# A convolution in four blocks beside an FFN: a loaded spectrum used twice, and a spectrum kept in the tile of the normalised x

## The chip, the cores and the metric

The kernel runs on one core of a Trainium2 chip. The metric is the device time of one execution in microseconds (us). Before the change it is 1384.04 us, the median of 3 runs (1380.11 to 1387.81). Several engines work side by side on the core, each with its own queue of instructions in a fixed order: TensorE (PE) multiplies matrices into PSUM, VectorE (DVE) and ScalarE (ACT) do elementwise work, GpSimd (POOL) and SyncE (SP) here mostly issue transfers between memory and the on-chip buffers.

## The reference

One input x of 2048 tokens with 576 features goes through two residual parts, each behind a layernorm with a scale and a shift (`ca`, `sa`, `ga` and so on come from a small product of `c` with `w_mod`):

```
h = layernorm(x) * (1 + ca) + sa
x = x + ga * (irfft(rfft(h, 4096) * rfft(K, 4096))[:2048] + h * D_skip)
h = layernorm(x) * (1 + cb) + sb
x = x + gb * (relu(h @ w1) @ w2)
```

The convolution runs along the tokens, one kernel K (2048 long) for each feature, built from the parameters `log_A_real`, `A_imag`, `C_real`, `C_imag` and `log_dt`. `w1` is 576 x 4608, `w2` is 4608 x 576. All is float32.

## The kernel before

The tokens are cut into four blocks of 512 (NB = 4). The convolution of block s needs block s and all earlier ones: it is a sum over t = 0 to s of products of a spectrum of K with a spectrum of block t of the normalised x. `conv(s)` (lines 847 to 953) does this in two halves of the features, p = 0 and 1:

- `norm1` writes the normalised x into `h` (a tile with the tag "h", one buffer, 2304 floats for each partition, in a pool `hb` of its own).
- `transform` multiplies it on PE with a matrix of cosines and sines (`ps_f`), ACT copies the result to `Z`, and `butterfly` on DVE makes `W` and then the spectrum `U_s_p`; the same for the piece of K, then `K_s_p`. Every operation of DVE in these helpers has line 509.
- `spec_K` also loads `R`, the spectrum of the piece of K before (from `Rd[s-1][p]`), and makes `K2` out of R and K (lines 887 and 889).
- `product(p, Y)` sums over pairs (Ka, Ua) in the order t = 0, s, 1, ..., s-1. For each pair it makes `T = Ka*Ua` and `Y = Y +- T` on DVE; the first pair writes two of its four products straight to Y. What is not at hand is loaded: `Ka` from `Kd` (`Kd[0]` is the same memory as `Rd[0]`) and `Ua` from `Ud`.
- `back` makes `V` from Y, `inverse` multiplies it on PE (`ps_i`, line 983, one PSUM buffer), and DVE adds each of the four results to x. Then `norm2` prepares the block for the FFN.

All spectra, Z, W, Y and V, and the loaded R, Ka and Ua, are tiles with the tag "S" (1152 KB) in a pool with 6 buffers (line 728). A tile takes the next buffer of the six and waits until its former owner has been read for the last time, by a store too. `load` (line 736) and `save` (line 740) are transfers issued by POOL.

The FFN of a block runs through 36 steps. Step g does `first(g)`: 14 matmuls into a PSUM tile `hps` (line 1284, two buffers), ACT makes `hh`, the relu rounded (line 1289), DVE makes the rest `hl` from hps and hh (line 1290), which frees the hps. Two steps later `second` does 14 matmuls of hh and hl with w2 into five accumulators (line 1309). During the first block DVE also splits each weight into a high and a low part (`w<-r,w`, line 509: one operation of 640 columns for w1; two, of 64 and 512, for w2), and SP stores the low parts for the later blocks (`L1d`, `L2d`, line 1364).

`conv(1)` runs beside the FFN of block 0, `conv(2)` beside that of block 1, `conv(3)` beside that of block 2; `conv(s)` is a generator out of which the FFN draws a few operations at each half step. The scheduler of the language then sets the order of each engine's queue, by priorities and by the times that it reckons with, so that a change of what an operation waits for can change the order too.

Of the kernel before, what the change touches and what calls it, by code (L numbers as in the profile page):

```python
# [10 lines left out]
F32 = mybir.dt.float32  # L11
# [7 lines left out]
P = 128  # L19
# [4 lines left out]
NB = 4  # L24
# [5 lines left out]
PC = 288  # L30
# [456 lines left out]
class Body:  # L487
# [359 lines left out]
    def conv(self, s):  # L847

        nc = self.nc
        v = nc.vector.tensor_tensor  # L850
        xp = self.xp[s % 2]
        x2 = self.x2p[s % 2].tile([P, 4, D], F32, tag="x2", bufs=1, name=f"x2_{s}")
        self.x2[s] = x2
        nc.gpsimd.dma_start(out=x2, in_=self.I["x"][s].rearrange("n m d -> m n d"))
        kt = [self.load_kt(s, 0), None]
        yield -1
        yield -1
        if s > 1:
            self.h = self.hb.tile([P, 4, D], F32, tag="h", name=f"h_{s}")
        h = self.h  # L860
        hv = h.rearrange("m n (dd p q) -> m n dd p q", dd=4, p=2)

        def mm_U(p, Z):
            return self.transform(lambda n2: hv[:, n2, :, p], self.fcU, Z)

        def mm_K(p, Z):
            ktv = kt[p].rearrange("p (t dd g) q -> p t dd g q", t=2, g=2)
            return self.transform(lambda n2: ktv[:, n2 // 2, :, n2 % 2], self.fcK, Z)

        def spec_U(p, Z):  # L870
            U = self.spec(f"U_{s}_{p}")
            yield from self.butterfly(Z, U, -1)
            yield -1
            if s + 1 < NB or p == 1:
                self.save(self.Ud[s][p], U)
            Us.append(U if p == 0 else None)

        def spec_K(p, Z):
            R = self.load(self.Rd[s - 1][p], "R")
            K = self.spec(f"K_{s}_{p}")  # L880
            yield from self.butterfly(Z, K, -1)
            yield -1
            if s + 1 < NB:
                self.save(self.Rd[s][p], K)
            f = nc.vector.scalar_tensor_tensor
            K2 = self.spec(f"K2_{s}_{p}")
            f(K2[:, :, 0], R[:, :, 1], self.sgn[:, 1:2], K[:, :, 0], op0=ALU.mult, op1=ALU.add)
            yield 1.35
            f(K2[:, :, 1], R[:, :, 0], self.sgn[:, 0:1], K[:, :, 1], op0=ALU.mult, op1=ALU.add)
            yield 1.35  # L890
            yield -1
            if s + 1 < NB:
                self.save(self.Kd[s][p], K2)
            Ks.append(K2)

        def product(p, Y):
            def pair(t):
                Ka = Ks[p] if t == 0 else self.load(self.Kd[s - t][p], "Ka")
                Ua = Us[p] if (t == s and Us[p] is not None) else self.load(self.Ud[t][p], "Ua")
                return Ka, Ua  # L900

            order = [0, s, *range(1, s)]
            nxt = pair(0)
            yield -1
            for i, t in enumerate(order):
                Ka, Ua = nxt
                if i + 1 < len(order):
                    nxt = pair(order[i + 1])
                yield from self.product(Y, Ka, Ua, i == 0)

        def inverse(p, V):
            ops = lambda n2: [(self.gc[:, n2, c, :], V[:, n2, c]) for c in range(2)]
            return self.inverse(x2, p, ops)

        def back(p, Y):
            V = self.spec(f"V_{s}_{p}")
            yield from self.butterfly(Y, V, 1)
            Vs.append(V)

        Us, Ks, Vs = [], [], []  # L920
        if s == 1:
            ZU = self.spec("Z")
            yield from mm_U(0, ZU)
            Z1 = self.spec("Z")
            yield from both(spec_U(0, ZU), mm_U(1, Z1))
            ZK = self.spec("Z")
            yield from both(spec_U(1, Z1), mm_K(0, ZK))
            kt[1] = self.load_kt(s, 1)
            yield from spec_K(0, ZK)
            ZK = self.spec("Z")  # L930
            Y = self.spec(f"Y_{s}_0")
            yield from both(product(0, Y), mm_K(1, ZK))
        else:
            ZK = self.spec("Z")
            yield from both(self.norm1(x2, h), mm_K(0, ZK))
            kt[1] = self.load_kt(s, 1)
            ZU = self.spec("Z")
            yield from both(spec_K(0, ZK), mm_U(0, ZU))
            Z1 = self.spec("Z")
            yield from both(spec_U(0, ZU), mm_U(1, Z1))  # L940
            ZK = self.spec("Z")
            yield from both(spec_U(1, Z1), mm_K(1, ZK))
            Y = self.spec(f"Y_{s}_0")
            yield from product(0, Y)
        yield from back(0, Y)
        yield from both(spec_K(1, ZK), after(3, inverse(0, Vs[0])))
        Y = self.spec(f"Y_{s}_1")
        yield from product(1, Y)
        yield from back(1, Y)
        yield -1  # L950
        yield -1
        yield from inverse(1, Vs[1])
        yield from self.norm2(s, x2, xp)
# [510 lines left out]
def after(n, g):  # L1464

    for _ in range(n):
        yield 0.0
    yield from g


def both(a, b):

    while True:
        n = 0
        for g in (a, b):
            for w in g:
                n = 1
                yield w
                break
        if not n:  # L1480
            return
# [58 lines left out]
```

## Time and profile before

| | us |
|---|---|
| median of 3 runs | 1384.04 (1380.11 to 1387.81) |
| the profiled execution | 1382.06 |
| its span in the profile | 1380.3 |
| PE busy | 1233.1 |
| DVE busy | 869.9 |
| ACT busy | 503.1 |
| POOL busy | 197.9 |

The profile is one execution, recorded by the hardware. Rows of a timeline give the start and the length in us, the engine, the line, the operation with what it writes and reads, and in brackets how long the engine was idle before and what ended that. "x2" means two such instructions in a row. Rows of waits give the sum, the number of times and the longest. The row of a window gives busy times and counts of PE, PE's weight loads, DVE, ACT and POOL, then the granted clock of PE as a share of full speed, the busy share of the DMA engines and GB/s. The mean clock over the span is 0.939. Where the FFN of block 0 runs with `conv(1)` beside it, up to about 565 us, DVE is the busier engine; from about 640 us on PE is busy nearly all the time.

### The profile page before, as it was taken

The page shows a single profiled execution, that of the slowest core. Times are in us where ns is not written, and L with a number is a line of the kernel's source. Part 1 is how long each engine was busy: PE and PEld are TensorE (multiplying, and loading weights), DVE is VectorE, ACT ScalarE, POOL GpSimd, SP SyncE. Part 2 cuts the span into 40 slices and gives each one's busy share as a digit, 9 for nine tenths or more (in the row PEclk, how much of TensorE's full clock was granted, in tenths as well). Part 3 has the DMA queues.
Part 4 walks back from the last instruction along what each step waited for, and adds up shares of the span by engine and source line. Part 5 has one row for each costly group of instructions (what it writes and reads, how often), then busy time and mean ns, then how long its engine had stood idle before and what let it go on. Part 6 is the DMA issues. An engine that isn't in the chain of part 4 may idle for free.

```text
span 1380.3 us, 26042 instructions
## 1 busy us (share of the span) xinstructions
PE 1233.1 (89%) x10608; PEld 977.5 (71%) x10608; DVE 869.9 (63%) x1351; ACT 503.1 (36%) x1014; POOL 197.9 (14%) x275
## 2 busy tenths in 40 slices
PE   5124778999999987989999999999999999999998
PEld 3123556777777766667777877777877878888886
DVE  5976977999886698559834987264999232111111
ACT  7985233222224322522234324433322253222231
POOL 1776222111121100021010010000010000000000
PEclk9555787999999999899999999999999999999999
DMA  6666399788888949598788995676998657666651
GB/s 193 240 242 239 101 331 364 271 314 306 283 317 282 334 157 337 164 353 316 238 279 304 323 369 179 204 240 210 365 323 299 202 152 212 198 198 193 205 172 60
DMA packets 134568, 347.55 MB, mean 252 GB/s; under 512 B 22448, under 2 KB 22768, under 8 KB 134448
## 3 DMA queue, kind: packets, MB, share of 16 engines
q1 hardware_dynamic: 106256, 218.36, 48.6%
q0 software_dynamic: 27904, 126.94, 25.2%
q8 instruction: 83, 1.36, 0.4%
q10 hardware_dynamic: 288, 0.59, 0.1%
q14 instruction: 37, 0.30, 0.1%
HBM read 264.44 MB, written 81.40 MB: 251 GB/s over the span
## 4 chain that ended last, share of the span: by engine, by line
PE 67%; DVE 18%; DMA 7%; issue 5%; ACT 3%; POOL 1%; SPq 0%; DVEq 0%; ACTq 0%; POOLq 0%
PE acc L1309 25%; PE hps L1284 25%; PE kps L440 5%; DVE Y L509 4%; PE ps_f L749 4%; DVE T L509 4%; PE kps L262 3%; DMA Ua<-Ud 2%; PE ps_i L983 2%; DVE W L509 2%; DMA Ud<-U 1%; DVE k L133 1%; DVE hl L1290 1%; PE kps L606 1%; DMA wm_gb<-in_w_mod_dram 1%
## 5 line engine op out<-in xcount | busy, mean ns | idle before, releaser
L1309 PE MATMUL acc<-hh,w 128*128 128x512 f32 x1296 | 424.2, 401 | 6.2 <-DVE w L509 6.1
L1284 PE MATMUL hps<-xh,w 128*128 128x512 f32 x1152 | 392.0, 400 | 0.6 <-issue 0.4
L1309 PEld LDWEIGHTS acc<-hh,w 128*128 128x128 f32 x1296 | 243.0, 189 | 60.3 <-DVE w L509 7.8
L1309 PE MATMUL acc<-hl,w 128*128 128x512 f32 x720 | 278.9, 399 | 0.0
L1290 DVE SCALAR_TENSOR_TENSOR hl<-hps,hh 128x512 fp32r<-128x512 f32 x144 | 98.7, 686 | 281.5 <-ACT hh L1289 281.4
L1284 PEld LDWEIGHTS hps<-xh,w 128*128 128x128 f32 x1152 | 214.8, 188 | 47.1 <-ACT xh L1046 1.1
L1284 PE MATMUL hps<-xl,w 128*128 128x512 f32 x576 | 229.0, 397 | 0.2 <-DVE xl L1051 0.2
L1289 ACT ACTIVATE hh<-hps 128x512 fp32r<-128x512 f32 x144 | 86.0, 597 | 336.4 <-PE hps L1284 335.9
L1262 ACT ACTIVATE w<-r 128x576 fp32r<-128x576 f32 x144 | 98.7, 686 | 219.1 <-issue 172.5
L1309 PEld LDWEIGHTS acc<-hl,w 128*128 128x128 f32 x720 | 135.3, 188 | 28.3
L1284 PEld LDWEIGHTS hps<-xl,w 128*128 128x128 f32 x576 | 108.2, 188 | 24.4 <-DVE xl L1051 1.2
L1255 ACT ACTIVATE w<-r 128x640 fp32r<-128x640 f32 x142 | 104.0, 732 | 18.7 <-DMA r<-in_w_dram 18.6
L262 PE MATMUL kps<-W,W 128*32 128x16 f32 x2304 | 40.0, 218 | 78.1 <-POOL W L59 49.7
L1284 PE MATMUL hps<-xs,w 128*128 128x512 f32 x288 | 95.5, 412 | 5.4 <-DVE hl L1290 5.4
L262 PEld LDWEIGHTS kps<-W,W 128*32 128x32 f32 x2304 | 37.6, 151 | 82.7 <-POOL W L59 51.0
L440 PEld LDWEIGHTS kps<-W1r,W2r 128*32 128x32 f32 x3456 | 69.0, 146 | 31.7 <-issue 17.6
L509 DVE TENSOR_TENSOR Y<-Y,T 128x1152 f32<-128x1152 f32 x64 | 84.9, 1349 | 0.2
L440 PE MATMUL kps<-W1r,W2r 128*32 128x48 f32 (+2 forms) x3456 | 78.3, 238 | 7.3 <-DVE W1r L412 4.2
L750 ACT ACTIVATE Z<-ps_f 128x288 f32<-128x288 f32 x104 | 42.4, 408 | 64.3 <-PE ps_f L749 63.7
L1284 PEld LDWEIGHTS hps<-xs,w 128*128 128x128 f32 x288 | 52.6, 188 | 18.3 <-DVE hl L1290 7.1
L509 DVE TENSOR_TENSOR w<-r,w 128x512 fp32r<-128x512 f32 (+2 forms) x108 | 57.9, 571 | 8.7 <-ACT w L1262 8.7
L509 DVE TENSOR_TENSOR W<-Z 128x576 f32<-128x576 f32 x52 | 37.0, 751 | 28.9 <-ACT Z L750 28.9
(214 smaller groups left out, 1381.7 us busy)
## 6 DMA issues: line engine op xcount, KB each, us to landing
r<-in_w_dram SPq DMA_DIRECT2D x144, 320.0 KB, 4.4
r<-in_w_dram SPq DMA_DIRECT2D x144, 288.0 KB, 3.8
w<-L1d SPq DMA_DIRECT2D x108, 320.0 KB, 3.0
w<-L2d SPq DMA_DIRECT2D x108, 288.0 KB, 3.2
W2r<-W2d POOLq DMA_DIRECT2D x18, 1536.0 KB, 9.3
W2d<-W SPq DMA_DIRECT2D x12, 1536.0 KB, 7.8
Ua<-Ud POOLq DMA_DIRECT2D x15, 1152.0 KB, 11.1
W<-W1d POOLq DMA_DIRECT2D x18, 768.0 KB, 8.9
```

The lines of the kernel that those rows point to most:

```text
L262: self.nc.tensor.matmul(ps[32 * dd : 32 * dd + 32, 12 * u + q, :], W2[:, r, :, ch], W1[:, u, :, r, ch], start=(r == 0), stop=(r == 1),)
L440: nc.tensor.matmul(ps[32 * dd : 32 * dd + 32, q, :], W2[:, r, :, ch], W1[:, :na, r, ch], start=(r == 0), stop=(r == 1),)
L509: return self.kept(self.nc.vector.tensor_tensor(*args, **kw))
L749: kept(nc.tensor.matmul(o, fc[:, n2, c, :], src(n2), start=True, stop=True))
L750: nc.scalar.activation(Z[:, n2, c], ps[:, :PC], AF.Copy)
L983: self.nc.tensor.matmul(ps[:, :PC], a, b, start=(i == 0), stop=(i == len(todo) - 1))
L1255: nc.scalar.activation(w[:, 0], r, AF.Copy)
L1262: nc.scalar.activation(w[:, 0:D], r2[g], AF.Copy)
L1284: nc.tensor.matmul(ps, a, x, start=(i == 0), stop=(i == 13))
L1289: nc.scalar.activation(hh, ps, AF.Relu)
L1290: nc.vector.scalar_tensor_tensor(hl, ps, 0.0, hh, op0=ALU.max, op1=ALU.subtract)
L1309: nc.tensor.matmul(acc[i], a, x, start=(f == 0 and j in (0, 3, 6, 9, 12)), stop=(f == NF - 1 and j in (2, 5, 8, 11, 13)),)
```

## The change

Three things change, all in `conv(s)`. First, in block 1 (s = 1) the second pair's Ka is the same memory as the R that `spec_K` has loaded; R is now kept and used, and nothing is loaded. Second, for each s the U of the second half (p = 1) is made in a tile of the tag "h", where the normalised x lay until the transforms had read it, and stays there for `product(1)`, which loaded it again from `Ud` before. It takes no buffer of the pool of six any more. Third, U_3_1 is no longer stored, as nobody loads it.

```
         def spec_U(p, Z):
-            U = self.spec(f"U_{s}_{p}")
+            if p:
+                U = self.hb.tile([P, 4, 2, PC], F32, tag="h", name=f"U_{s}_{p}")
+            else:
+                U = self.spec(f"U_{s}_{p}")
             yield from self.butterfly(Z, U, -1)
             yield -1
-            if s + 1 < NB or p == 1:
+            if s + 1 < NB:
                 self.save(self.Ud[s][p], U)
-            Us.append(U if p == 0 else None)
+            Us.append(U)
 
         def spec_K(p, Z):
             R = self.load(self.Rd[s - 1][p], "R")
+            Rs.append(R)
...
             def pair(t):
-                Ka = Ks[p] if t == 0 else self.load(self.Kd[s - t][p], "Ka")
-                Ua = Us[p] if (t == s and Us[p] is not None) else self.load(self.Ud[t][p], "Ua")
+                if t == 0 or s == 1:
+                    Ka = (Rs if t else Ks)[p]
+                else:
+                    Ka = self.load(self.Kd[s - t][p], "Ka")
+                Ua = Us[p] if t == s else self.load(self.Ud[t][p], "Ua")
                 return Ka, Ua
...
-        Us, Ks, Vs = [], [], []
+        Us, Ks, Rs, Vs = [], [], [], []
```

The order of the queues moves with it, in three places. Lines after the change are 4 to 7 higher than before (hl is line 1297, hps 1291, acc 1316, ps_i 990).

DVE, second half of block 1, from the x add of the first half's last `ps_i` on; before, `Ua_5956` is the first pair's U, `hl_6049` and `hl_6108` belong to steps 31 and 32 of the FFN:

```order
L509 TENSOR_TENSOR x2_1_5272<-ps_i_5944,x2_1_5272 128x4x72
L509 TENSOR_TENSOR T_5996<-K2_1_1_5913,Ua_5956 128x1152
L509 TENSOR_TENSOR T_6006<-K2_1_1_5913,Ua_5956 128x1152
L509 TENSOR_TENSOR w1_5995<-r1_5958,w1_5995 128x640
L1290 SCALAR_TENSOR_TENSOR hl_6049<-hps_6030,hh_6048 128x512
L509 TENSOR_TENSOR w2_6080<-r2_5960,w2_6080 128x64
L509 TENSOR_TENSOR w2_6080<-r2_5960,w2_6080 128x512
L509 TENSOR_TENSOR w1_6052<-r1_6018,w1_6052 128x640
L509 TENSOR_TENSOR Y_1_1_5955<-K2_1_1_5913,Ua_5956 128x4x288 x2
L509 TENSOR_TENSOR Y_1_1_5955<-Y_1_1_5955,T_5996 128x4x288
L509 TENSOR_TENSOR Y_1_1_5955<-Y_1_1_5955,T_6006 128x4x288
L1290 SCALAR_TENSOR_TENSOR hl_6108<-hps_6086,hh_6107 128x512
```

The same place after; `hl_6043` belongs to step 31, and R and U_1_1 are read where Ka and a second Ua were loaded:

```order
L509 TENSOR_TENSOR x2_1_5272<-ps_i_5942,x2_1_5272 128x4x72
L509 TENSOR_TENSOR Y_1_1_5953<-K2_1_1_5911,Ua_5954 128x4x288 x2
L509 TENSOR_TENSOR T_5990<-K2_1_1_5911,Ua_5954 128x1152
L509 TENSOR_TENSOR T_6000<-K2_1_1_5911,Ua_5954 128x1152
L509 TENSOR_TENSOR Y_1_1_5953<-Y_1_1_5953,T_5990 128x4x288
L509 TENSOR_TENSOR Y_1_1_5953<-Y_1_1_5953,T_6000 128x4x288
L509 TENSOR_TENSOR T_6010<-R_5846,U_1_1_5471 128x1152
L509 TENSOR_TENSOR w1_5989<-r1_5956,w1_5989 128x640
L509 TENSOR_TENSOR Y_1_1_5953<-Y_1_1_5953,T_6010 128x4x288
L509 TENSOR_TENSOR T_6033<-R_5846,U_1_1_5471 128x1152
L1297 SCALAR_TENSOR_TENSOR hl_6043<-hps_6024,hh_6042 128x512
```

The hl of step 31 stood behind two products and one w; now it stands behind nine products and one w. The hl of step 32 follows five more products, three w and four W later.

PE at the same place, before (`hps_6144` is the first half of step 33; it takes the PSUM buffer of step 31, which hl_6049 frees):

```order
L1309 MATMUL acc4_0_3041<-hl_5992,w2_5964 128x512
L1284 MATMUL hps_6144<-xs_0_2781,w1_5995 128x512 x2
L1284 MATMUL hps_6144<-xh_0_2779,w1_5995 128x512
L1284 MATMUL hps_6144<-xl_0_2780,w1_5995 128x512
L1284 MATMUL hps_6144<-xh_0_2779,w1_5995 128x512 x2
L1284 MATMUL hps_6144<-xl_0_2780,w1_5995 128x512
L1284 MATMUL hps_6144<-xh_0_2779,w1_5995 128x512 x2
L1284 MATMUL hps_6144<-xl_0_2780,w1_5995 128x512
L1284 MATMUL hps_6144<-xh_0_2779,w1_5995 128x512 x2
L1284 MATMUL hps_6144<-xl_0_2780,w1_5995 128x512
L1284 MATMUL hps_6144<-xh_0_2779,w1_5995 128x512
L1309 MATMUL acc0_0_3037<-hh_6048,w2_6024 128x512 x2
```

And after (`hps_6138` is step 33, which takes the PSUM buffer that hl_6043 frees):

```order
L1316 MATMUL acc4_0_3041<-hl_5986,w2_5962 128x512
L1316 MATMUL acc0_0_3037<-hh_6042,w2_6018 128x512 x2
L1316 MATMUL acc1_0_3038<-hh_6042,w2_6018 128x512 x2
L1316 MATMUL acc2_0_3039<-hh_6042,w2_6018 128x512 x2
L1316 MATMUL acc3_0_3040<-hh_6042,w2_6018 128x512 x2
L1316 MATMUL acc4_0_3041<-hh_6042,w2_6018 128x512
L1291 MATMUL hps_6138<-xs_0_2781,w1_5989 128x512 x2
```

Nine matmuls with the hh of step 31 now come ahead of the hps of step 33, and those with its hl behind it.

DVE in block 2, at the end of `spec_K(1)` where the first half's result is added to x; before:

```order
L887 SCALAR_TENSOR_TENSOR K2_2_1_8558<-R_8489,sgn_203,K_2_1_8491 128x4x288
L1290 SCALAR_TENSOR_TENSOR hl_8541<-hps_8521,hh_8540 128x512
L509 TENSOR_TENSOR x2_2_7715<-ps_i_8546,x2_2_7715 128x4x72
L889 SCALAR_TENSOR_TENSOR K2_2_1_8558<-R_8489,sgn_203,K_2_1_8491 128x4x288
L509 TENSOR_TENSOR x2_2_7715<-ps_i_8560,x2_2_7715 128x4x72
```

And after:

```order
L891 SCALAR_TENSOR_TENSOR K2_2_1_8552<-R_8483,sgn_203,K_2_1_8485 128x4x288
L893 SCALAR_TENSOR_TENSOR K2_2_1_8552<-R_8483,sgn_203,K_2_1_8485 128x4x288
L1297 SCALAR_TENSOR_TENSOR hl_8535<-hps_8515,hh_8534 128x512
L509 TENSOR_TENSOR x2_2_7709<-ps_i_8540,x2_2_7709 128x4x72
L509 TENSOR_TENSOR x2_2_7709<-ps_i_8554,x2_2_7709 128x4x72
```

The first x add now stands behind both K2 operations instead of one. On POOL, the Ka of block 2's second pair is now issued ahead of the store of U_2_1, which came first before. In block 3 the last two x adds of the first half stand one product later, and the last `ps_i` three matmuls later.

## The prediction

> **What bounds the kernel now.** I read the page's first part first, then the waits of PE in stretches, then the timelines around the waits. First the busy times of the whole span:
>
> ```profile
> PE 1233.1 (89%) x10608; PEld 977.5 (71%) x10608; DVE 869.9 (63%) x1351; ACT 503.1 (36%) x1014; POOL 197.9 (14%) x275
> ```
>
> PE is busy for 89% of 1380.3 us, so a time can only be won where PE is idle or slow. The change touches the convolutions of blocks 1 to 3, which run beside the FFN of blocks 0 to 2. These are all the waits of PE that matter there (line, what it waited for, us, times, longest), for the stretches 440 to 600, 565 to 640, 780 to 850 and 1000 to 1080:
>
> ```profile
> PE acc L1309 <- DVE w L509: 6.1, 3, 5.4
> PE hps L1284 <- DVE hl L1290: 5.0, 3, 2.0
> PE ps_i L983 <- DVE V L509: 2.6, 1, 2.6
> ...
> PE kps L440 <- DVE W1r L412: 4.2, 1, 4.2
> ...
> PE ps_i L983 <- DVE x L509: 3.4, 1, 3.4
> ...
> PE ps_i L983 <- DVE x L509: 3.1, 2, 2.1
> ```
>
> PE waits for DVE every time, never for one of the transfers that the change removes. So a removed load or store counts only as far as DVE stood still for it and PE stood still for DVE afterwards. DVE's own idle times (the bracket) beside the spectra, from its timeline:
>
> ```profile
> 480.58 2.63 DVE L509 TENSOR_TENSOR Y<-K,Ua 128x1152 f32<-128x1152 f32 x2 [5.27 <-issue]
> 526.28 2.63 DVE L509 TENSOR_TENSOR T<-K,Ua 128x1152 f32<-128x1152 f32 x2 [2.88 <-DMA Ua<-Ud]
> 540.81 2.63 DVE L509 TENSOR_TENSOR T<-Ka,Ua 128x1152 f32<-128x1152 f32 x2 [3.43 <-issue]
> 750.67 2.63 DVE L509 TENSOR_TENSOR T<-K,Ua 128x1152 f32<-128x1152 f32 x2 [4.27 <-DMA Ua<-Ud]
> 756.61 1.36 DVE L509 TENSOR_TENSOR Y<-K,Ua 128x1152 f32<-128x1152 f32 x1 [3.31 <-DMA Ud<-U]
> 962.35 2.63 DVE L509 TENSOR_TENSOR T<-K,Ua 128x1152 f32<-128x1152 f32 x2 [5.32 <-DMA Ua<-Ud]
> 967.55 2.63 DVE L509 TENSOR_TENSOR Y<-K,Ua 128x1152 f32<-128x1152 f32 x2 [1.97 <-DMA Ud<-U]
> ```
>
> Which of the seven does the change remove? 480.58, 526.28, 750.67 and 962.35 wait for the Ua of the first pair, which is still loaded. 540.81 waits for Ka and Ua of block 1's second pair: both loads go. 756.61 and 967.55 wait for the store of U_2_1 and U_3_1: Y_2_0 and Y_3_0 took the buffer that the store was reading; U_s_1 no longer lies in that pool.
>
> **The change part by part.** Six transfers of 1152 KB go: two Ka and one Ua in block 1, one Ua each in blocks 2 and 3, one store in block 3. DVE's arithmetic stays.
>
> *Block 1, first half.* Only the Ka behind the Ua goes. Issue times on POOL, and microseconds to landing from the DMA view:
>
> ```profile
> 469.43 0.76 POOL L736 DMA_DIRECT2D Ua<-Ud  x1
> 470.18 0.75 POOL L736 DMA_DIRECT2D Ka<-Rd  x1
> ```
> ```profile
> Ua<-Ud POOLq DMA_DIRECT2D x1, 1152.0 KB, 11.1
> Ka<-Rd POOLq DMA_DIRECT2D x1, 1152.0 KB, 14.7
> ```
>
> Ua lands at 480.5, Ka at 484.9, 4.4 us behind: one after the other, not side by side. Without Ka, Ua lands when it did, and DVE starts at 480.58 as before. Bounds: 0, and 4.4 if they shared the engines; I take 0.
>
> *Block 1, second half.* Here the order moves more than the transfers. DVE from the first two products (526.28, above) on, and PE, before:
>
> ```profile
> 528.82 0.82 DVE L509 TENSOR_TENSOR w<-r,w 128x640 fp32r<-128x640 f32 x1
> 529.56 0.69 DVE L1290 SCALAR_TENSOR_TENSOR hl<-hps,hh 128x512 fp32r<-128x512 f32 x1
> ...
> 551.11 2.75 DVE L509 TENSOR_TENSOR W<-Y 128x576 f32<-128x576 f32 x4
> 553.78 2.89 DVE L509 TENSOR_TENSOR V<-W 128x576 f32<-128x576 f32 x6
> 556.59 1.41 DVE L509 TENSOR_TENSOR w<-r,w 128x512 fp32r<-128x512 f32 x2
> ```
> ```profile
> 532.06 0.62 PE L1284 MATMUL hps<-xs,w 128*128 128x512 f32 x2
> ...
> 535.23 0.61 PE L1309 MATMUL acc<-hh,w 128*128 128x512 f32 x2
> ...
> 544.75 1.07 PE L1309 MATMUL acc<-hh,w 128*128 128x512 f32 x4
> 551.24 0.80 PE L1309 MATMUL acc<-hh,w 128*128 128x512 f32 x1 [5.42 <-DVE w L509]
> 554.67 2.26 PE L983 MATMUL ps_i<-V,gc 128*128 128x288 f32 x4 [2.64 <-DVE V L509]
> 557.33 2.07 PE L1309 MATMUL acc<-hh,w 128*128 128x512 f32 x4 [0.40 <-DVE w L509]
> ...
> 560.36 0.84 PE L1284 MATMUL hps<-xs,w 128*128 128x512 f32 x2
> ```
>
> A product takes 1.27 us ((528.82-526.28)/2), a half step of the FFN 3.17 (535.23-532.06, 14 matmuls, 0.226 each). In the new order nine products and one w of 0.74 stand between 526.28 and the hl of step 31: 526.28 + 9 x 1.27 + 0.74 + 0.69 = 539.1. PE has nine matmuls with hh left after 532.06, until 534.1; then hps of step 33 waits for the PSUM buffer that this hl frees: 5.0 us, not there before. It goes on to 539.1 + 2 x 3.17 = 545.4. The hl of step 32 stands behind five more products, three w (1.41 and about 0.15) and the four W: 539.1 + 6.35 + 1.56 + 2.75 + 0.69 = 550.4; PE waits 5.0 again, less what slow matmuls fill. At 550.4 it has still to do, up to where it stood at 560.36 before: 14 + 5 + 9 matmuls (6.3) and two ps_i groups of about 0.75, 558.2; I add 1.2 for short waits on the x adds and half-filled starts: 559.4. So the 3.43 us that DVE saves become 1.0 us on PE. The two waits sum to 10 where 5.4, 2.6 and 0.4 stood; V comes some 2.7 us sooner, and PE has done less by then. Bounds: 3.4 gained if the whole saving reaches PE, 1.8 lost by slow matmuls, as follows.
>
> What happens after a wait of 5 us the rows show: four acc matmuls took 2.07 at 557.33 and 1.07 at 544.75. The four rows at 554.67 and 557.33 and what lies around them cost some 2.8 us of slowness (2.26 - 1.13 for the ps_i, 2.07 - 1.07 for the acc, the rest in the ps_i after them). Of the two new waits, the tail of the first lies inside the second and costs nothing; the second, cut to about 2.2 by it, is near the longest wait of block 3 (2.1, above), behind which block 3's rows, further down, show nearly whole matmuls. A second full tail of 2.8 would turn the gain of 1.0 into a loss of 1.8, the lower bound.
>
> The Trainium skill (TensorE: Matmul & The Clock Gate, Part 1: The HAM clock gate) says that an idle window of about 3.4 us halves TensorE's clock and that as long a busy stretch restores it. The trace agrees: the granted clock of 540 to 560 is 0.74.
>
> ```profile
> 540.00:560.00 20.00, 11.55 (x37) 8.10 (x36) 18.89 (x25) 3.11 (x5) 0.00 (x0) 0.74 0.49 161
> ```
>
> By that rule the change sets two waits of 5.0 where one of 5.4 was, and the second, if it is not cut, makes the sum 1.9 us instead of 4.7; the rows leave both open, and I keep 1.0.
>
> *After block 1*, PE has no wait between 560 and 604, so the earlier x adds (some 4 us) win nothing there; the wait of 4.2 at kps stands behind output stores and moves along with PE: 0. SP's store of each w now waits some 7 us longer for DVE; behind it are loads of r that are used three steps (3 x 6.35) later: 0.
>
> *Block 2.* 3.31 us of DVE's idle time go. It ends at:
>
> ```profile
> 798.48 0.44 DVE L509 TENSOR_TENSOR x<-ps_i,x 128x288 f32<-128x288 f32 x1
> 798.85 1.40 DVE L889 SCALAR_TENSOR_TENSOR K<-R,sgn,K 128x1152 f32<-128x1152 f32 x1
> ```
> ```profile
> 798.98 2.29 PE L983 MATMUL ps_i<-V,gc 128*128 128x288 f32 x4 [3.42 <-DVE x L509]
> 800.65 1.47 PE L1309 MATMUL acc<-hh,w 128*128 128x512 f32 x2
> ...
> 1034.65 1.24 PE L983 MATMUL ps_i<-V,gc 128*128 128x288 f32 x4 [2.07 <-DVE x L509]
> ...
> 1043.59 1.24 PE L983 MATMUL ps_i<-V,gc 128*128 128x288 f32 x4 [1.01 <-DVE x L509]
> ```
>
> Between 757 and 798 DVE never idles, so the 3.31 travel down, unless an hl has to wait for its hh. The nearest such pair:
>
> ```profile
> 779.85 0.60 ACT L1289 ACTIVATE hh<-hps 128x512 fp32r<-128x512 f32 x1 [2.43 <-PE hps L1284]
> ```
> ```profile
> 784.38 0.68 DVE L1290 SCALAR_TENSOR_TENSOR hl<-hps,hh 128x512 fp32r<-128x512 f32 x1
> ```
>
> 784.38 - 780.45 = 3.9 us of slack, more than 3.31. But the first x add now stands behind one more K operation (1.33): it comes 2.0 us earlier, and PE's 3.42 becomes 1.4. The four ps_i rows took 2.29 after it, against 1.24 after a wait of 2.07 in block 3 (1034.65); some 2 us of slowness followed with the acc at 800.65. After a wait of 1.4 most of it should go: I take 0.5 of the 2 only, since the second ps_i has its own wait coming. Gain 2.5, from 0.5 (the next Ua late by 1.5) to 4.
>
> *Block 3.* 1.97 go; the idle time before the x adds moves along. The first of the two waits quoted last falls to about 0.1. The third x add stands one product (1.27) later in the order, so it comes 0.7 earlier, and the last ps_i with it: the two together win 0.7, and three matmuls (0.7) more lie ahead of that ps_i. Gain 1.2 (0 to 2.5).
>
> **Sum:** 1.0 + 2.5 + 1.2 = 4.7 us. The profiled execution took 1382.06 (span 1380.3), so 1377.4; the median of the runs shown is 1384.04, 2 us above, so I forecast 1379.3, 0.34% faster. About 0.5% (6.9 us) is what a measurement of this kernel can tell from no change; this lies within it.
>
> **The rivals.** *Faster: DVE's idle time comes through whole.* 3.43 + 3.31 + 1.97 = 8.7, and with it the slow matmuls behind 551.24 and 798.98 (2.8 + 2), 13.5 in all: 1370.5. For it: each of these waits has a wait of PE behind it. Against it: the new order in block 1 holds the hl back. It decides from the point where the first wait of PE in block 1 stays under some 3 us. A rule goes further: were the queue's transfers shared packet by packet, the Ua at 480.58 would come up to 4.4 sooner; the landings 4.4 apart speak against it. The Trainium skill (DMA: Bandwidth & Descriptors, Queues, rings and completion order) tells of sharing between queue rows and of ring order within one; the landings agree with the second.
>
> *Slower: the hl of steps 31 and 32 behind the products.* Place: DVE's row between Ua's landing at 526 and W. Price: at 550.4 PE is 6.3 us of FFN work behind, where before it had done all but the ps_i; if V then comes no sooner than before (a Ua that lands 3 us later, or slow splits of w), PE pays the 6.3, with a new slow tail in place of the old; blocks 2 and 3 give their low ends, 0.5 + 0: 1384.0 + 5.8 = 1389.8. Another 1.2 us, such as a slow tail in block 2 that stays and grows, puts it past 0.5%. It decides once the two waits together exceed 12 us.
>
> *Nothing: the idle times are taken up by the next wait.* Block 1's 1.0 is lost in the second wait, block 2's wait for x is replaced by a wait for the next Ua: 0 to 1.5 gained, 1383. For it: between 560 and 604 PE waits for nothing, so what comes earlier there is worth nothing.
>
> That the change does not do what it says I give nearly nothing: the new order shows no load of those six.
>
> **How the numbers follow.** The forecast (1375 to 1383) 0.50; nothing 0.17; faster rival 0.20, slower rival 0.13. The forecast's own range crosses 1377.1 with a tenth of its chance at the lower end (block 1 at 3.4, block 2 at 4): 0.05 and more of the whole, so faster 0.27; slower by over 0.5% (over 1391) needs the slower rival with its extra: 0.10 with the unforeseen; the rest, 0.63, is within. The range from 1371 to 1388 takes in the faster rival's better half and most of the slower one.
>
> **What would show it.** Right: in block 1 no idle time of DVE before the pair with R; a wait of PE of about 5 us for an hl at 534; no wait for the store in blocks 2 and 3; ps_i at 799 waiting 1 to 2 us with fast matmuls behind it. Wrong: the Ua of the first pair landing earlier (queue shared); hl of step 31 ahead of the products; a sum of PE's waits in blocks 1 to 3 that falls by more than 8 us or rises.

## The result and the profile after

The changed kernel takes 1375.01 us, the median of 6 runs (1368.68 to 1376.59), beside 1382.99 us (6 runs) before: a ratio of 0.9934, with a 95% interval from 0.991 to 0.9957. By the ratio that is 9 us (the two medians are 8.0 apart), nearly twice the 4.7 that were forecast; it lies inside the range, but beyond the 0.5% within which the likeliest case saw it. The profiled execution has a span of 1374.8 us.

The busy times of PE, DVE and ACT are those of before within 1.4 us, so what is gone is waiting:

```profile
PE 1232.8 (90%) x10608; PEld 978.1 (71%) x10608; DVE 871.3 (63%) x1351; ACT 503.5 (37%) x1014; POOL 194.3 (14%) x269
```

These are PE's waits in the stretches 440 to 640, 780 to 850 and 1000 to 1080:

```profile
PE hps L1291 <- DVE hl L1297: 10.7, 5, 4.9
PE kps L440 <- DVE W1r L412: 2.4, 1, 2.4
PE kps L440 <- issue: 2.2, 1, 2.2
...
PE ps_i L990 <- DVE V L509: 2.1, 1, 2.1
...
PE ps_i L990 <- DVE x L509: 0.3, 1, 0.3
```

In block 1 the waits for w and V have given way to waits for hl, as forecast. In blocks 2 and 3 the waits for x (3.4, and 3.1 in two) are gone but for 0.3, and a wait for V of 2.1 is new. In all, PE's waits in these stretches fall from 24.4 to 17.7 us.

A span holds some noise of its own: its first part, up to the first mark below, in which the kernels hardly differ, ends between 470 and 484 us in the twelve traces. So I compare stretches between four marks, the times at which ACT makes the hh of one step: step 26 in the FFN of block 0, step 19 of blocks 1 and 2, step 20 of block 3. Between them lie `conv(1)`'s end with the preparation that follows it, `conv(2)` and `conv(3)`; I call the stretches block 1, 2 and 3. The marks before:

```profile
479.24 0.60 ACT L1289 ACTIVATE hh<-hps 128x512 fp32r<-128x512 f32 x1 [0.35 <-PE hps L1284]
...
744.15 0.60 ACT L1289 ACTIVATE hh<-hps 128x512 fp32r<-128x512 f32 x1 [1.20 <-PE hps L1284]
...
1014.14 0.60 ACT L1289 ACTIVATE hh<-hps 128x512 fp32r<-128x512 f32 x1 [2.44 <-PE hps L1284]
...
1266.91 0.60 ACT L1289 ACTIVATE hh<-hps 128x512 fp32r<-128x512 f32 x1 [2.44 <-PE hps L1284]
```

And after:

```profile
481.62 0.60 ACT L1296 ACTIVATE hh<-hps 128x512 fp32r<-128x512 f32 x1 [0.34 <-PE hps L1291]
...
744.61 0.60 ACT L1296 ACTIVATE hh<-hps 128x512 fp32r<-128x512 f32 x1 [1.20 <-PE hps L1291]
...
1011.62 0.60 ACT L1296 ACTIVATE hh<-hps 128x512 fp32r<-128x512 f32 x1 [2.44 <-PE hps L1291]
...
1261.40 0.60 ACT L1296 ACTIVATE hh<-hps 128x512 fp32r<-128x512 f32 x1 [2.44 <-PE hps L1291]
```

The stretches were 264.9, 270.0 and 252.8 us long; now they are 263.0, 267.0 and 249.8. So 1.9 + 3.0 + 3.0 = 7.9 us are won in the trace, against 1.0 + 2.5 + 1.2 in the forecast.

Of the 1.9 us of block 1, only 0.9 are won by step 9 of its FFN. The other 1.0 falls in steps 9 to 13, where PE waits for nothing in either kernel; these are the four steps before and after:

```profile
651.53:692.12 40.59, 40.59 (x738) 31.50 (x739) 33.17 (x46) 10.68 (x24) 5.62 (x9) 1.00 0.71 239
```
```profile
653.03:692.59 39.56, 39.56 (x738) 31.18 (x739) 31.84 (x44) 10.66 (x23) 5.02 (x8) 1.00 0.71 243
```

PE's queue has another order there, a fourth place where the order moves: its small matmuls of line 440 stand between those of the FFN in other groups. Those four steps take 40.6 us in the kernel before and in kernels 1, 2, 5 and 6 below, and 39.5 to 39.6 us in the changed kernel and in 3, 4, 7, 8, 9 and 10. So 1.0 to 1.1 us of a difference in the column of block 1 can come from there.

Where blocks 2 and 3 win more is seen on POOL, in the time at which the first pair's Ua is issued. Before, with DVE's last reading of the second half's Z ahead of each issue:

```profile
741.56 1.43 DVE L509 TENSOR_TENSOR W<-Z 128x576 f32<-128x576 f32 x2 [4.05 <-ACT Z L750]
743.53 0.76 POOL L736 DMA_DIRECT2D Ua<-Ud  x1 [10.90 <-ACT Z L750]
...
952.19 1.43 DVE L509 TENSOR_TENSOR W<-Z 128x576 f32<-128x576 f32 x2 [5.67 <-ACT Z L750]
954.14 0.76 POOL L736 DMA_DIRECT2D Ua<-Ud  x1 [47.59 <-ACT w L1255]
```

And after, with DVE's first products of the two blocks below:

```profile
733.08 0.76 POOL L736 DMA_DIRECT2D Ua<-Ud  x1
743.99 0.76 POOL L736 DMA_DIRECT2D Ka<-Rd  x1 [10.16 <-ACT Z L750]
...
937.23 0.76 POOL L736 DMA_DIRECT2D Ua<-Ud  x1 [33.20 <-issue]
```
```profile
746.89 2.63 DVE L509 TENSOR_TENSOR Y<-K,Ua 128x1152 f32<-128x1152 f32 x2
...
954.53 2.63 DVE L509 TENSOR_TENSOR Y<-K,Ua 128x1152 f32<-128x1152 f32 x2
```

Ua waited for a buffer of the six. In both blocks its issue came 0.5 us after DVE had read that Z (at 742.99 and 953.62), so I take it for the buffer of Z; the traces do not name the buffers, and the bracket names ACT. With U_s_1 out of that pool Ua takes a buffer that is free sooner, by 11 and 14 us when each is counted from the mark behind it, and the Ka behind it waits in its place (0.5 us after the same reading). So beside the 3.3 and 2.0 us that the forecast counted, DVE's waits of 4.27 and 5.32 for Ua are gone too: both rows have no bracket.

### The profile page after: what moved, and what is told of

It is laid out like the page before. It is cut to its first block, busy times and chain, and to the rows that moved or that the text cites. A ratio compares the mean times of both kernels' runs of the same rounds, so it can differ in the third digit from the quotient of the medians.

```text
span 1374.8 us, 26052 instructions
## 1 busy us (share of the span) xinstructions
PE 1232.8 (90%) x10608; PEld 978.1 (71%) x10608; DVE 871.3 (63%) x1351; ACT 503.5 (37%) x1014; POOL 194.3 (14%) x269
## 4 chain that ended last, share of the span: by engine, by line
PE 69%; DVE 14%; DMA 8%; issue 6%; ACT 2%; POOL 1%; SPq 0%; DVEq 0%; ACTq 0%; POOLq 0%
PE hps L1291 26%; PE acc L1316 26%; PE kps L440 5%; PE ps_f L749 4%; PE kps L262 3%; DVE T L509 3%; DVE Y L509 2%; PE ps_i L990 2%; DMA Ua<-Ud 2%; DVE k L133 1%; DMA h<-in_x_dram 1%; DMA Ka<-Rd 1%; DMA L1d<-w 1%; DVE W L509 1%; PE kps L606 1%
## 5 line engine op out<-in xcount | busy, mean ns | idle before, releaser
L1291 PE MATMUL hps<-xh,w 128*128 128x512 f32 x1152 | 396.2, 403 | 1.0 <-issue 0.9
L1291 PEld LDWEIGHTS hps<-xh,w 128*128 128x128 f32 x1152 | 218.5, 191 | 49.4 <-ACT xh L1053 1.5
```

The lines of the kernel that those rows point to most:

```text
L1291: nc.tensor.matmul(ps, a, x, start=(i == 0), stop=(i == 13))
```

## The experiments

The table gives, for each kernel, the ratio to the kernel before with its interval, and how much longer each stretch is in its trace than before (us). Theory F says that blocks 2 and 3 win by the freed buffer; theory O, that in block 1 the order of the hl takes back what the loads gave. Where the order and the loads of a block are those of before (blocks 2 and 3 in 3, 8 and 10, block 1 in 2), its stretch still differs by up to 1.0 us; less than that is not read.

| kernel | ratio | block 1 | block 2 | block 3 |
|---|---|---|---|---|
| the change | 0.9934 (0.991 to 0.9957) | -1.9 | -3.0 | -3.0 |
| 1: U in h, loaded again | 0.9988 (0.9965 to 1.0011) | +1.2 | +1.2 | -2.2 |
| 2: blocks 2 and 3 alone | 0.994 (0.9915 to 0.9964) | -1.0 | -3.4 | -3.5 |
| 3: block 1 alone | 0.9972 (0.9951 to 0.9993) | -3.6 | +0.6 | -0.8 |
| 4: block 1's pairs swapped | 0.9872 (0.9837 to 0.9908) | -11.0 | -3.1 | -2.8 |
| 5: hl sooner | 0.9896 (0.9862 to 0.9931) | -0.6 | -3.2 | -3.6 |
| 6: 4 and 5 together | 0.9819 (0.9784 to 0.9854) | -14.3 | -3.8 | -2.4 |
| 7: U_3_1 stored | 0.9925 (0.9896 to 0.9954) | -3.2 | -2.7 | -3.6 |
| 8: pairs swapped in the kernel before | 1.0031 (1.0008 to 1.0053) | +5.2 | -0.7 | +0.3 |
| 9: U_2_1 loaded again | 0.9968 (0.9942 to 0.9993) | -1.9 | -2.2 | -3.0 |
| 10: R kept alone | 1.001 (0.9983 to 1.0036) | +0.8 | +0.7 | +1.0 |

**1. U_s_1 in the tile of h, but stored and loaded as before, and block 1's Ka loaded too.**

```
-            if s + 1 < NB:
+            if s + 1 < NB or p == 1:
                 self.save(self.Ud[s][p], U)
-            Us.append(U)
+            Us.append(U if p == 0 else None)
...
-                if t == 0 or s == 1:
-                    Ka = (Rs if t else Ks)[p]
+                if t == 0:
+                    Ka = Ks[p]
...
-                Ua = Us[p] if t == s else self.load(self.Ud[t][p], "Ua")
+                Ua = Us[p] if (t == s and Us[p] is not None) else self.load(self.Ud[t][p], "Ua")
```

> U_s_1 lies in the tile of h, but is stored and loaded again as before, and block 1's Ka is loaded again: all transfers of before are made. Theory F (the buffer that U_s_1 no longer takes from the six lets the first pair's Ua be loaded sooner in blocks 2 and 3): 5 to 6 us faster than before, DVE's waits for Ua of 4.3 (block 2) and 5.3 (block 3) gone, block 1 as before. Rival T (what counts is the traffic that is gone): within 1.5 us of before, the 4.3 and 5.3 still there.

Each theory had half of it. In time nothing is won that can be told from noise (0.9988, with 1 inside the interval), where F expected 5 to 6 us. But DVE's waits for the first Ua are gone and so is PE's wait for x near 798, and block 3 wins 2.2 us. Block 2 as a whole loses: up to step 31 of its FFN it is 5.0 us ahead, then it gives back 6.1, at the second half, where Ka and, behind it, U_2_1 come from memory. DVE and PE there:

```profile
817.67 2.63 DVE L509 TENSOR_TENSOR T<-Ka,Ua 128x1152 f32<-128x1152 f32 x2 [4.51 <-DMA Ua<-Ud]
```
```profile
843.34 2.26 PE L990 MATMUL ps_i<-V,gc 128*128 128x288 f32 x4 [3.21 <-DVE V L509]
844.99 1.04 PE L1316 MATMUL acc<-hl,w 128*128 128x512 f32 x1
845.82 1.06 PE L1291 MATMUL hps<-xs,w 128*128 128x512 f32 x2
```

The changed kernel has the same place with a wait of 2.06, and gives back 2.0:

```profile
811.39 2.63 DVE L509 TENSOR_TENSOR T<-Ka,U 128x1152 f32<-128x1152 f32 x2 [2.54 <-DMA Ka<-Rd]
```
```profile
837.66 1.21 PE L990 MATMUL ps_i<-V,gc 128*128 128x288 f32 x4 [2.06 <-DVE V L509]
838.50 0.61 PE L1316 MATMUL acc<-hh,w 128*128 128x512 f32 x1
```

So the 6.1 are a wait of 3.2 and 2.9 of slow matmuls behind it (two hps matmuls 1.06 instead of 0.63; the granted clock is 0.50 from 842.18 to 849.01); the 2.0 are a wait alone.

**2. The change in blocks 2 and 3 alone**, with `if p and s > 1:` ahead of the tile of h, and Ka and U_1_1 loaded in block 1.

> The change in blocks 2 and 3 alone. F: 5 to 6 us faster than before (3 for each block), block 1's waits of PE as before (5.4 and 2.6). Rival B (most of the time comes from block 1): 2 us or less.

Blocks 2 and 3 win 6.9 us in the trace and 8 in the timing, more than was expected, and block 1's waits are those of before (5.1 for w, 2.6 for V). Theory B falls.

**3. The change in block 1 alone**, with `if p and s == 1:` instead.

> The change in block 1 alone. F: 1.5 to 2 us faster than before, with the wait of about 5 us for hl of step 31 and about 2 for that of step 32; blocks 2 and 3 as before (3.4 and 2.1). Rival B: 5 us or more.

3.6 us in block 1, where 1.5 to 2 were expected; the waits for hl are 11.6 in all, 5.1 the longest. The four traces that have block 1's new code (the change, 3, 7 and 9) give 1.9, 3.6, 3.2 and 1.9, a mean of 2.7. The two of 1.9 (the change and 9) have a stretch of half clock behind the second of the long waits for hl (553.52 to 556.93 in the change); the other two have none. Blocks 2 and 3 stay within 0.8 of before. The parts add up: 0.994 x 0.9972 = 0.9912, beside 0.9934 with its interval.

**4. Block 1's pairs swapped:** the pair with R and U_1, both at hand, first.

```
-            order = [0, s, *range(1, s)]
-            nxt = pair(0)
+            order = [1, 0] if s == 1 else [0, s, *range(1, s)]
+            nxt = pair(order[0])
```

> The change, and in block 1 the pair t = 1 (R and U_1, both at hand) ahead of the pair t = 0 (whose Ua is loaded). If the load of Ua still costs PE time in block 1: DVE's idle times of 5.1 and 2.8 ahead of the first pairs gone, the wait for hl of step 31 under 2 us, 3 to 6 us faster than the changed kernel. Rival (block 1 is bound by DVE's own work between the splits and the products, the idle only moves): within 1.5 us of the changed kernel.

More than expected: 11.0 us in block 1, 9 beyond the changed kernel, though two signs came only in part: DVE still waits 2.90 for the first half's Ua, and PE 2.82 for an hl where under 2 was expected. In the changed kernel DVE's first pair waits in both halves:

```profile
482.81 2.63 DVE L509 TENSOR_TENSOR Y<-K,Ua 128x1152 f32<-128x1152 f32 x2 [5.11 <-issue]
...
528.42 2.63 DVE L509 TENSOR_TENSOR Y<-K,Ua 128x1152 f32<-128x1152 f32 x2 [2.82 <-DMA Ua<-Ud]
```

The first half of kernel 4 shows what changes. DVE makes two products of the pair with R at 447.54 and the other four operations of it from 461.90 on, while Ua is loaded, and waits 2.90 for Ua behind them instead of 5.11 ahead of everything:

```profile
461.90 2.62 DVE L509 TENSOR_TENSOR Y<-R,U 128x1152 f32<-128x1152 f32 x2
...
470.70 2.63 DVE L509 TENSOR_TENSOR T<-K,Ua 128x1152 f32<-128x1152 f32 x2 [2.90 <-DMA Ua<-Ud]
```

In the second half DVE does not wait for a load at all. PE's waits for hl fall from five, 10.7 us in all, to one of 2.82:

```profile
529.87 1.22 PE L1291 MATMUL hps<-xs,w 128*128 128x512 f32 x2 [2.82 <-DVE hl L1297]
...
531.31 2.12 PE L990 MATMUL ps_i<-V,gc 128*128 128x288 f32 x4
```

So in block 1 the wait for the first Ua still held everything back: of DVE's 5.11 + 2.82 us of idle time 2.90 are left. The order of the hl moves with the swap as well, so how much of the 9 us is the wait for Ua and how much the waits for hl that went with it is not separated.

**5. The hl sooner.** In block 1's second half each pair is written a half step later, so that the scheduler takes the hl of step 31 behind six products instead of nine:

```
+                if s == 1 and p == 1 and True:
+                    yield -1
                 yield from self.product(Y, Ka, Ua, i == 0)
```

> The change, with the products of block 1's second half written later by up to two half steps, so that in DVE's order the hl of step 31 stands behind six products instead of nine, and that of step 32 ahead of the four W. Theory O (the order of the hl takes back most of what block 1 could win): the wait of PE for the hl of step 31 falls from 4.9 to about 1, V comes when it came, and the kernel is 1 to 4 us faster than the changed one. Rival (PE is only made to wait elsewhere, for V): within 1 us of it.

PE's wait for that hl falls from 4.85 to 2.45 (1 was expected), and the hps matmuls behind it run whole, 0.73 instead of 1.22:

```profile
534.17 0.73 PE L1293 MATMUL hps<-xs,w 128*128 128x512 f32 x2 [2.45 <-DVE hl L1299]
```

From the first mark to step 3 of block 1's FFN the kernel wins 3.1 us on before, where the changed kernel wins 0.9; but at the second mark 0.6 are left. The rest is lost in the preparation that follows conv(1). These are steps 3 to 9, in this kernel and in the changed one:

```profile
592.12:649.89 57.77, 52.28 (x702) 41.09 (x703) 44.61 (x40) 13.05 (x23) 8.85 (x13) 0.94 0.96 346
```
```profile
597.78:653.03 55.25, 50.64 (x703) 39.86 (x704) 46.03 (x43) 13.07 (x24) 8.11 (x12) 1.00 0.97 355
```

PE waits 4.37 and 1.09 there, with half clock from 608.63 to 615.46, where the changed kernel waits 2.45 and 2.16 at full clock; 1.0 more goes in steps 9 to 13, whose order is that of before. The timing is 0.38% below the changed kernel's, with intervals that overlap, while the trace shows nothing won in the end. Theory O is right about the wait; whether the kernel gains by it alone is left open.

**6. Both together.**

> Both: in block 1 the pair at hand first, and its products written later as in the run before. O: the wait of 2.8 for an hl at the end of block 1 goes, 1 to 3 us faster than the kernel with the swapped pairs alone. Rival: within 1 us of that.

No wait for hl is left in block 1, and the stretch is 3.3 us shorter than in 4 (4.4 up to step 9; the order of steps 9 to 13 takes 1.1 back). The ratio is 0.9819 (0.9784 to 0.9854), beside 0.9872 (0.9837 to 0.9908) for 4. It has the lowest ratio of the study, 25 us below before and some 16 below the changed kernel; from 4 the timing alone does not tell it clearly, as the intervals still overlap.

**7. U_3_1 stored, for nobody**, with `or p == 1` behind `s + 1 < NB`.

> The change, but U_3_1 is stored as before, from the tile of h, and nobody reads it. If block 3 won by the buffer: the same time as the changed kernel within 1 us, with at most a wait of 2 on DVE for the Ka that queues behind the store. Rival (block 3 won by the store that is gone from the queue): 2 to 3 us slower, block 3's waits of PE for x back at 2 and 1.

As F expected: DVE waits 2.14 for the Ka behind the store, and block 3 wins 3.6 us all the same.

```profile
960.67 2.63 DVE L509 TENSOR_TENSOR T<-Ka,U 128x1152 f32<-128x1152 f32 x2 [2.14 <-DMA Ka<-Rd]
```

So the store that is gone is worth nothing that can be measured in block 3.

**8. The pairs swapped in the kernel before.**

> The kernel before, with block 1's pairs swapped and nothing else: the first pair then needs a loaded Ka and a loaded Ua. If the swap wins only because R and U_1 are at hand: no gain, within 2 us of before, DVE still idle 5 us or more ahead of the first pair. Rival (the swap wins by the order of the instructions alone): 5 us or more faster than before.

Neither: it is 0.31% slower, by 5.2 us in block 1. The first products wait 5.30 for Ka, as expected, so the swap alone does not hide the load. The loss is in the second half, where the order puts a part of w that the acc needs behind all fourteen products in a row; in the kernel before, w and hl stood between them, and the wait was 5.4:

```profile
559.17 0.80 PE L1309 MATMUL acc<-hh,w 128*128 128x512 f32 x1 [11.20 <-DVE w L509]
562.61 2.26 PE L983 MATMUL ps_i<-V,gc 128*128 128x288 f32 x4 [2.64 <-DVE V L509]
```

**9. U_2_1 loaded again**, in block 2 alone.

```
-                Ua = Us[p] if t == s else self.load(self.Ud[t][p], "Ua")
+                Ua = Us[p] if t == s and (s, p) != (2, 1) else self.load(self.Ud[t][p], "Ua")
```

> The change, but in block 2 alone U_2_1 is loaded again for the second half's product, as before, although it lies in the tile of h (its store is there in both). If the load that is gone is what block 2's second half wins by: 3 to 5 us slower than the changed kernel, with PE's wait for V near 840 us up from 2.1 to about 3.2 and slow matmuls behind it. Rival (the run with all transfers lost there for another reason): within 1 us of the changed kernel.

The wait comes as expected, 2.82 for V, but the slow matmuls do not: the stretch is only 0.8 us longer than in the changed kernel.

```profile
842.59 1.21 PE L990 MATMUL ps_i<-V,gc 128*128 128x288 f32 x4 [2.82 <-DVE V L509]
843.42 0.61 PE L1316 MATMUL acc<-hl,w 128*128 128x512 f32 x1
```

The timing says 0.9968, 0.34% above the changed kernel, with intervals that overlap. So the load of U_2_1 costs about 1 us by itself, no more than the noise of a stretch, and some 4 where half clock follows the wait that it causes, as in 1. The last section shows that this is not decided by the wait's length alone.

**10. R kept, nothing else** (U_s_1 in the pool of six, stored and loaded).

> R is kept and used in block 1, nothing else: U_s_1 lies in the pool of six, is stored and loaded as before in all blocks. The order of block 1's second half is that of the changed kernel, with one load of U_1_1 more. If blocks 2 and 3 win by U alone: within 2.5 us of before, PE's waits near 798 and 1034 us at 3.4 and 2.1 as before, and DVE's idle times of 4.3 and 3.3 in block 2 there. Rival (keeping R out of the rotation of the buffers is enough to win there too): 4 us or more faster.

No gain. Blocks 2 and 3 have their waits back, one for x of 4.3 and two of 4.1 in all, and in DVE 4.58 for Ua and 3.23 for the store. In block 1 DVE's order is the changed kernel's but for the first four products, and U_1_1 is loaded, and PE's longest wait for hl is 7.4 instead of 4.9:

```profile
PE hps L1288 <- DVE hl L1294: 13.4, 4, 7.4
...
PE ps_i L987 <- DVE x L509: 4.3, 1, 4.3
...
PE ps_i L987 <- DVE x L509: 4.1, 2, 3.1
```

So R kept alone wins nothing in block 1, and blocks 2 and 3, which do not use it, win by U_s_1 in the tile of h. In block 1 U_1_1 in the tile of h but loaded again wins nothing either (1); the two together win (3). No run keeps U_1_1 at hand and loads Ka, so what R adds to it is not shown.

## Why the prediction was right or wrong

**What bounds the kernel** held: PE's waits are for DVE, and only what let DVE go sooner counted. The store of U_3_1 gone is worth nothing by itself (7).

**Which idle times go** is the step that failed. The prediction said that 750.67 and 962.35 "wait for the Ua of the first pair, which is still loaded", and kept them. It asked whether the load was still there, and not what the load itself was waiting for. The row of POOL at 743.53, idle for 10.90 us and issued as soon as a Z had been read, had that answer, a buffer, and the change frees one. Runs 1, 2 and 7 show it: in all of them the 4.27 and 5.32 are gone, with the transfers put back or not, while in 3 (4.11 and 3.92) and 10 (4.58 and 6.66), with U_2_1 and U_3_1 in the pool, they stand. These two terms the forecast put at nothing. In the trace blocks 2 and 3 came out 0.5 and 1.8 us above it; the other 0.9 of the shortfall is block 1's.

**Block 1** came out as described: 4.85 us for the hl of step 31 (5.0 forecast), 1.93 for that of step 32 (2.2 after the slow matmuls), V's ps_i at 553.21. The term was 1.0; measured are 1.9 in the profile, of which 0.9 lie where the forecast looked and 1.0 in steps 9 to 13, where it did not, and 2.7 in the mean of four traces. The rows:

```profile
541.33 1.22 PE L1291 MATMUL hps<-xs,w 128*128 128x512 f32 x2 [4.85 <-DVE hl L1297]
...
552.41 0.73 PE L1291 MATMUL hps<-xs,w 128*128 128x512 f32 x2 [1.93 <-DVE hl L1297]
...
553.21 1.88 PE L990 MATMUL ps_i<-V,gc 128*128 128x288 f32 x4
```

The tail of the first wait lies inside the second, as forecast. The second wait's own tail the forecast put at nothing, as a wait of 2.07 in block 3 had none; here it has one (the ps_i takes 1.88 instead of 1.13), in 9 too, in 3 and 7 not, so that the 0.9 came near the 1.0 partly by luck. That the Ua would land no sooner without the Ka behind it held: from its issue to DVE's start it took 11.15 us before (469.43 to 480.58) and 10.99 after (471.82 to 482.81). But that wait, which the forecast left as it was, was still a large cost of block 1: run 4, which puts the pair at hand ahead of it, wins 9 us more.

**Block 2** was 2.5 forecast and 3.0 measured, by another sum: the wait of 3.42 with all of its tail is gone at 798 (5.0), not half; and 2.0 are given back by a wait for V at 837 that was not foreseen. It comes from the Ka that DVE waits 2.54 us for (811.39), whose load is queued behind another and two stores. That the two numbers are near is luck.

**Block 3** was 1.2 forecast and 3.0 measured: both waits for x (2.07 and 1.01) are gone but for 0.31, since DVE came to its first products at 954.53 instead of 962.35, which is 5.3 us sooner beside the 2.5 by which everything was ahead; the forecast had only the 2.0 of the store, which come on top. Nor do the 0.7 and 0.7 that the prediction names for this block add up to its 1.2.

**The rivals.** The faster one had the right direction and the wrong place: its 13.5 us contained block 1's whole saving, which did not come, and left out the two waits for Ua that did. The slower one and "nothing" did not occur: the two long waits for hl sum to 6.8 us, not 12, and PE's waits fell by 6.7 us in all, within the 8 that the prediction allowed. In a kernel like 8, a part of w behind all the products, the order does cost more than it wins, though.

## What to carry to other kernels

When a tile leaves a pool whose buffers are taken in turn, look at every load from the pool behind it: ask what its issue waits for now, and which buffer it will get, before asking whether its bytes are still moved. Where a sum has one part at hand and one that must be loaded, begin with the part at hand: here that was worth as much again as the whole change, while the swap without a part at hand lost time (8). And after a change to what a product waits for, read the new order of the small operations that the other engine waits for; here three products fewer ahead of one took 2.4 us off the wait of PE, though the kernel's time did not clearly follow.

## What the runs showed of the hardware

Whether TensorE's matmuls are slow after a wait is not settled by the length of the wait here. In the twelve traces the granted clock changes only at marks that are 3.41 us, or a multiple of it, apart, and slow stretches go with how long PE was busy between two marks. From 480 to 1100 us, every 3.41 us between two marks that had full clock and less than 1.5 us of busy PE (30 of them) were followed by 3.41 us at half clock; of those with 1.50 to 1.72 us it was 5 of 15, and of those with more none of some 2000. So a wait that lies between two marks can be punished (followed by half clock), and a longer one that a mark divides need not be. The first pair of rows below is from the changed kernel, around its wait of 1.93 us up to 552.41; the second from run 10, around a wait of 3.06 us up to 1037.31:

```profile
550.10:553.52 3.42, 1.49 (x7) 0.81 (x6) 3.42 (x6) 0.00 (x0) 0.00 (x0) 1.00 0.88 274
553.52:556.93 3.41, 3.41 (x9) 2.58 (x8) 3.41 (x10) 0.00 (x0) 0.00 (x0) 0.50 0.47 178
```
```profile
1032.58:1035.99 3.41, 1.67 (x8) 1.04 (x6) 3.31 (x4) 0.69 (x1) 1.49 (x2) 1.00 1.04 391
1035.99:1039.40 3.41, 2.09 (x9) 1.71 (x10) 3.41 (x4) 0.00 (x0) 0.00 (x0) 1.00 1.05 397
```

In the same way a wait of 2.82 us was punished in run 4 (1.49 us busy from 525.46 to 528.87) and one of 2.82 us was not in run 9 (1.64 us busy from 840.81 to 844.23). At half clock pairs of matmuls took 1.05 to 1.22 us instead of 0.63; so 3.41 us of it cost up to 1.7 us, an estimate (half of 3.41). The Trainium skill (TensorE: Matmul & The Clock Gate, HAM oscillation) warns of gaps of more than about 3.4 us; here a gap well below that was punished (one of 1.82 us in the changed kernel up to 502.12, with a clock of 0.50 from 502.32 to 505.73), and one of 3.06 us was not. So for a wait of 2 to 3 us the tail depends on where the marks fall, which differs from trace to trace, and a forecast has to carry it as a chance.
